# The router's early steps move ahead of the scores' minima in an attention and mixture-of-experts kernel

## The chip, the cores and the metric

One core of a Trainium2 chip runs the whole program. The metric is device microseconds of one execution, from start to end.

## What is computed

Attention over 8 batches and 8 heads with 576 positions of 64 numbers, a window of 128 positions and a bias that falls with the distance; its output, seen as 4608 tokens of 512 numbers, goes through a router that gives each token to one of 8 experts, and each expert is two matrix products with a ReLU between. The router sorts all (token, expert) logits downward and gives each token its expert while that has room:

```python
scores = np.where(mask, scale * np.matmul(q, k.transpose(0, 1, 3, 2)) + bias[None], -1000000000.0)
attn = np.exp(scores - np.max(scores, axis=-1, keepdims=True))
attn = attn / (np.sum(attn, axis=-1, keepdims=True) + 1e-09)
x = np.matmul(attn, v)          # as 4608 tokens x 512
...
logits = x @ w_gate             # 4608 x 8
for idx in np.argsort(-logits.flatten()):
    tok, e = (int(idx) // E, int(idx) % E)
    if assigned[tok] >= 0 or counts[e] >= cap:     # cap = 576
        continue
    assigned[tok] = e
    counts[e] += 1
...
h = np.maximum(x[mask] @ w1[e], 0.0)
out[mask] = h @ w2[e]
```

## The kernel before

`attention` runs over 32 pairs (a batch b and two heads), in a loop over n with four stages in each turn: the scores and minima of pair n, the turning of pair k = n - 2's weights, the product with `v` (`av`) of pair k - 1, and the last stage of pair k - 2. Nearly every instruction on TensorE (PE), VectorE and ScalarE is put in the order in which the code is written, so the order in the loop is the order in each engine's queue. One turn of the loop does, for the queues that matter here:

- VectorE: `least(n-1, 1)`, the minima of the second half of the scores (tile `u`, with the bias added); two copies `turned` of turned weights from PSUM into `PT`; `least(n, 0)`, the minima of the first half of the next scores; `divide(k-2)`, which makes `rs` (the reciprocals of the sums), `Lp` (parts of the logits) and `xb` (the output); and then, at the end, one early step of the router.
- PE: three turns into PSUM banks `pt`; `natural(k-2)`, which turns the product back and multiplies with the router's weights `wn`; the turns of tiles 0 and 4 into one more bank, for which PE waits until VectorE has copied the first `PT`; `scores(n, 0)`; `av(k-1)`; `scores(n, 1)`.
- ScalarE: the exponentials, one or two copies; GpSimd: sums `sd` of the denominators and, once per batch, the logits `L_sb` (lines L296 to L299).

The eight `pt`, `s` and `x` tiles fill PSUM: four banks `pt`, two `s`, two `x`.

The router needs all logits before it can choose, but parts of its work are done early. After batch b's logits, `early` puts generators on a list, and `early_step` takes one step of the first of them: `first_choice` in two halves (the best logit `b`, `ne` and `cand`; then its expert `am` and `OH`), and, once 27 of 36 token columns have their logits, `early_counts`: smallest and largest logit `ext`, their transpose on PE and `em`, `ed`; a matmul of `ed` that brings them to all partitions, and seven small instructions from `ev` to `hi`; the step width `w` and the places `kq`; then the indicator `ind` in three pieces and 13 matmuls that count. The steps fall in n = 8, 9, 12, 13, 16, 17, 20, 21, 24, 25, 28 and 29 (two halves for each of the six batches), n = 29 to 33 (`early_counts`); after n = 31 there are no more scores. In the profile all instructions of the steps have the line of the helper that records them, L446, and PE's matmuls L53.

Of the kernel before, what the change touches and what calls it, by code (L numbers as in the profile page):

```python
# [25 lines left out]
def attention(tc, pools, qk_in, v_in, rel_in, C, x_dram, L_sb, router):  # L26
# [25 lines left out]
    def mm(out, w, a, start=True, stop=True):  # L52
        put(nc.tensor.matmul(out, w, a, start=start, stop=stop, skip_group_check=True))  # L53

    def load(n):
        b, p = divmod(n, NP)
        t = sb.tile([128, QKW], F32, name="qk", bufs=3)
        nc.sync.dma_start(t, qk_in[b, p])
        state[n] = dict(q=t[:, 0:576], k=t[:, 576:1152])

    def load_v(n):
        b, p = divmod(n, NP)
        st = state[n]
        st["v"] = sb.tile([128, NB, 64], F32, name="v", bufs=4)
        nc.sync.dma_start(st["v"], v_in[b, p].rearrange("k (m c) -> k m c", c=64))

    def biases(p):

        bm[p] = pools["pp"].tile([128, BMW], F32, name=f"bm{p}")
        eng = nc.vector if p == 0 else nc.gpsimd  # L70
        for c0, c1 in ((0, 320), (320, 512)):
            for h in range(2):
                eng.tensor_scalar(bm[p][:, 512 * h + c0:512 * h + c1], rel[:, c0:c1], 2.0 ** -(2 * p + h + 1), 1.0, ALU.mult, ALU.mult)
            if c0 == 0:
                eng.tensor_scalar(bm[p][:, 1024:1216], rel[:, 0:192], rel[:, 512 + p:513 + p], 1.0, ALU.mult, ALU.mult)

    def unit(n, t):


        par = n // NP % 2  # L80
        m0, ms = 2 + par, 3 - 2 * par
        if t == 0:
            return m0, 0, 0, 320 if par else 192
        if t == 1:
            return 3, 64 * m0, 128 * m0, 0
        if t == 4:
            return ms, 64 * m0 + 192, 128 * m0 + 384, 1216 - 64 * ms
        return 3, 192 * (t - 2), 128 * m0 + 64 * ms + 384 * (t - 1), 0
# [9 lines left out]
    def keys(n, t, r):  # L98

        par = n // NP % 2  # L100
        qb = par + 2 * t + r if t < 4 else 8 - 8 * par
        if t == 0:
            return qb, 0, qb + 1
        return qb, max(0, qb - 2), min(3, qb + 1)

    def scores(n, half):
        st = state[n]
        q, k = st["q"], st["k"]
        if half == 0:
            st["u"] = sb.tile([128, 1600], F32, name="u", bufs=4)  # L110
            st["mn"] = sb.tile([128, 9], F32, name="mn", bufs=4)
            st["sm"] = sb.tile([128, 9], F32, name="sm", bufs=6)
        s = [bank() if half and n < 2 else ps_s.tile([128, 512], F32, name="s") for _ in range(2)]
        for t in UNITS[half]:
            m, c = unit(n, t)[0:2]
            w = 64 * m
            for h, r in HR if t < 4 else ((0, 0), (1, 1)):
                qb, kb, _ = keys(n, t, r)
                mm(s[h][hs[r], c:c + w], q[hs[h], 64 * qb:64 * qb + 64], k[hs[h], 64 * kb:64 * kb + w])
        st["s"] = s  # L120
# [41 lines left out]
    def turned(n, t, ps, copy):  # L162
        T = state[n][t] = sb.tile([128, 576], F32, name=f"PT{t}")
        w = 384 if t else place(n, 4, unit(n, 4)[0])
        put(copy(T[:, 0:w], ps[:, 0:w]))  # L165
# [43 lines left out]
    def copy_out(n):  # L209
        st = state[n]  # L210
        xT = st["xT"] = sb.tile([128, 640], F32, name="xT")
        for i, w in ((0, 320), (1, 256)):
            put(nc.scalar.copy(xT[:, 384 * i:384 * i + w], st["x"][i][:, 0:w]))

        nc.gpsimd.tensor_copy(xT[:, 320:384], xT[:, 256:320])

        st["sd"] = sb.tile([128, 10], F32, name="sd")
        add = nc.gpsimd.tensor_scalar
        add(st["sd"][:, 0:8], st["sm"][:, 0:8], 1e-9, 1.0, ALU.add, ALU.mult)
        for h in range(2):  # L220
            for r in range(2):
                add(st["sd"][hs[r], 8 + h:9 + h], st["sm"][hs[h], 8:9], 1e-9, 1.0, ALU.add, ALU.mult)
# [82 lines left out]
    NPAIRS = B * NP  # L305
# [7 lines left out]
    def bank():  # L313
        return ps_t.tile([128, 512], F32, name="pt")

    for n in range(NPAIRS + LAG + 2):
        if 0 < n < NPAIRS - 1:
            load(n + 1)
        if 0 < n <= NPAIRS:
            load_v(n - 1)  # L320
        if n == 2:
            nc.sync.dma_start(wn, C["wn_in"])
        if n == CONST_AT:
            load_consts(tc, pools["c"], C["cst_in"], C)
        if 0 < n < NP:
            biases(n)
        k = n - LAG
        turns, ends = 0 <= k < NPAIRS, 0 <= k - 2 < NPAIRS
        if ends:
            copy_out(k - 2)  # L330
        if 0 < n <= NPAIRS:
            least(n - 1, 1)
        if turns:
            ps = {}
            for t in (2, 1, 3):
                ps[t] = bank()
                turn(k, t, ps[t])
            turned(k, 2, ps[2], nc.scalar.copy)
        if 0 < n <= NPAIRS:
            exps(n - 1, 1)  # L340
        if turns:
            turned(k, 1, ps[1], nc.vector.tensor_copy)
            turned(k, 3, ps[3], nc.vector.tensor_copy)
            room = ps[3][:, 384:512]
        if k - 1 == NPAIRS - 1:
            av(k - 1)
        if ends:
            N = [bank(), bank()]
            natural(k - 2, N)
        if turns:  # L350
            ps = bank()
            turn(k, 0, ps)
            turn(k, 4, ps)
            turned(k, 0, ps, nc.scalar.copy)
        if n < NPAIRS:
            scores(n, 0)
            least(n, 0)
            exps(n, 0)
        if ends:
            divide(k - 2, N)  # L360
            if (k - 2) % NP == NP - 1 and k - 2 < NPAIRS - 1:
                logits((k - 2) // NP)
            if n < NPAIRS:
                router.early_step(room)
        if 0 <= k - 1 < NPAIRS - 1:
            av(k - 1)
        if n >= NPAIRS:
            for _ in range(1 if turns else 2):
                router.early_step(room if turns else None)
        if n < NPAIRS:  # L370
            scores(n, 1)

# [81 lines left out]
class Router:  # L454
# [24 lines left out]
    def bank(self):  # L479
        if self.room is not None:  # L480
            return self.room
        return self.p["ps_m"].tile([128, 512], F32, name="m")
# [116 lines left out]
    def early(self, c0, c1):  # L599

        choice = self.first_choice(self.L0, self.b0, self.am0, self.OH0, c0, c1)
        if c1 == NT:
            for steps in self.steps + [choice]:
                for _ in steps:
                    pass
            return
        self.steps += [iter([None]), choice]
        if c1 == FIRST:
            self.steps.append(self.early_counts())

# [11 lines left out]
    def early_counts(self):  # L622
        nc, rt, c1 = self.nc, self.p["rt"], FIRST - 1
        self.first = lo, w, rw = yield from self.ends(self.b0[:, 0:FIRST], True)
        self.clamp(self.c0, self.b0, lo, w, 0, c1)
        key = self.place(self.c0, lo, rw, 0, c1)
        ind = rt.tile([128, NT, J], BF, name="ind", bufs=1)
        yield
        for i in range(EARLY_CUTS):
            a, z = (c1 * j // EARLY_CUTS for j in (i, i + 1))  # L630
            self.indicate(ind, key, a, z)
        cnt = self.count(ind, self.OH0, 0, c1)
        t = self.small("pt", 8)
        nc.vector.tensor_copy(t[J:2 * J, :], cnt[0:J, 0:8])
        nc.vector.tensor_tensor(self.part[J:2 * J, :], cnt[J:2 * J, 8:16], t[J:2 * J, :], ALU.add)
# [328 lines left out]
def load_consts(tc, pool, cst, C):  # L964
    nc = tc.nc
    n = sum(w for _, w, _ in CONSTS)
    raw = pool.tile([128, n], F32, name="craw")
    nc.sync.dma_start(raw, cst)
    o = 0
    for k, w, dt in CONSTS:  # L970
        r = raw[:, o:o + w]
        if dt == F32:
            C[k] = r
        elif dt == BF:
            t = pool.tile([128, w], BF, name="c_" + k)
            nc.vector.tensor_copy(t, r)
            C[k] = t
        else:
            t = pool.tile([128, w, dt], BF, name="c_" + k)
            nc.vector.tensor_copy(t, bc(r.unsqueeze(2), [128, w, dt]))  # L980
            C[k] = t
        o += w
# [159 lines left out]
```

## Time and profile before

| | |
|---|---|
| Time, median of 3 runs | 717.23 us (717.13 to 718.87) |
| The profiled execution | 715.13 us, of which 713.4 us are the span from the first to the last instruction |
| Busy in the span: PE, VectorE, ScalarE, GpSimd | 679.1, 466.0, 331.1, 154.5 us |
| Attention | up to about 222 us |
| The router's first route, with PE mostly idle | from there to about 240 us |
| Experts | from there to the end |

The busy times are averages over parts with different limits. What a change in one part is worth is read in that part. PE's ends are modelled, so that PE's busy time is not PE at its peak.

### The profile page before, as it was taken

How to read it: one execution, taken by the hardware profiler on the slowest of the kernel's cores; microseconds unless marked ns; L12 is line 12 of the kernel's file. 1: busy time of each engine (PE TensorE's matmuls, PEld its weight loads, DVE VectorE, ACT ScalarE, POOL GpSimd, SP SyncE). 2: the span in 40 equal slices, each digit the busy share in tenths (PEclk: the TensorE clock that was granted, in tenths of full speed). 3: DMA queues.
4: the chain of work that ended last, by engine and by line, in shares of the span. 5: the costliest groups of instructions: out<-in, count | busy, mean ns of one | idle time of the engine just before them, and what ended most of it. 6: DMA issues, size and time to landing. Idle time of an engine off the chain costs nothing.

```text
span 713.4 us, 19210 instructions
## 1 busy us (share of the span) xinstructions
PE 679.1 (95%) x7447; PEld 596.6 (84%) x7447; DVE 466.0 (65%) x1855; ACT 331.1 (46%) x991; POOL 154.5 (22%) x337
## 2 busy tenths in 40 slices
PE   7999999999995699999999999999999999999996
PEld 4898888888874399789889889988988988988985
DVE  6778777877887789869578828846765724523210
ACT  6888888888873253324233223314324324322210
POOL 4121221221220301533042132132033023011011
PEclk9999999999997699999999999999999999999998
DMA  8465465465522352718135235135134334301001
GB/s 301 137 212 181 145 215 181 154 211 177 163 85 61 115 190 89 238 44 272 47 122 205 84 109 177 47 117 177 60 119 131 122 104 137 131 30 37 1 24 49
DMA packets 35140, 92.74 MB, mean 130 GB/s; under 512 B 3808, under 2 KB 13152, under 8 KB 35040
## 3 DMA queue, kind: packets, MB, share of 16 engines
q1 hardware_dynamic: 29152, 72.55, 31.0%
q0 software_dynamic: 5888, 18.88, 8.1%
q8 instruction: 61, 1.00, 0.6%
q14 instruction: 39, 0.32, 0.1%
HBM read 72.54 MB, written 18.87 MB: 128 GB/s over the span
## 4 chain that ended last, share of the span: by engine, by line
PE 76%; DVE 13%; DMA 4%; issue 4%; POOL 1%; SPq 1%; ACT 0%; POOLq 0%; DVEq 0%
PE ph L893 27%; PE po L922 10%; PE po L923 10%; PE po L925 8%; DVE u L133 6%; PE s L53 5%; PE pt L53 4%; PE pt L157 4%; PE x L53 3%; PE pg L870 2%; DVE xb L255 2%; PE m L579 1%; DMA craw<-in_cst_dram 1%; DVE PT L165 1%; DMA g<-x,idx 1%
## 5 line engine op out<-in xcount | busy, mean ns | idle before, releaser
L893 PE MATMUL ph<-xh,hl 128*128 128x288 f32 (+2 forms) x1024 | 192.0, 299 | 0.0
L893 PEld LDWEIGHTS ph<-xh,hl 128*128 128x128 f32 x1024 | 154.6, 189 | 1.0
L144 ACT ACTIVATE u<-u,mn 128x192 f32<-128x192 f32 (+2 forms) x288 | 123.8, 433 | 22.5 <-DVE mn L133 22.5
L922 PE MATMUL po<-hl,hh 128*128 128x512 f32 (+1 forms) x328 | 130.7, 399 | 0.0
L923 PE MATMUL po<-hl,hh 128*128 128x512 f32 (+1 forms) x328 | 126.4, 385 | 0.0
L893 PE MATMUL ph<-xl,hl 128*128 128x288 f32 (+2 forms) x512 | 115.9, 297 | 0.0
L899 ACT ACTIVATE hh<-ph 128x288 fp32r<-128x288 f32 (+2 forms) x128 | 46.6, 409 | 147.5 <-PE ph L893 141.4
L133 DVE CUSTOM_DVE_ANT_0 u<-s,bm 128x192 f32<-128x192 f32 x308 | 86.4, 333 | 39.5 <-PE s L53 39.0
L925 PE MATMUL po<-hl,hlo 128*128 128x512 f32 (+1 forms) x264 | 101.7, 385 | 0.0
L837 DVE TENSOR_TENSOR hl<-raw,hl 128x512 fp32r<-128x512 f32 x128 | 85.0, 683 | 14.4 <-ACT hl L835 13.9
L934 POOL DMA_INDIRECT out_dram<-o,idx x40 | 44.1, 1104 | 204.3 <-ACT o L929 120.9
L893 PEld LDWEIGHTS ph<-xl,hl 128*128 128x128 f32 x512 | 84.2, 189 | 0.1
L874 DVE TENSOR_TENSOR xl<-pg,xh 128x512 fp32r<-128x512 f32 (+1 forms) x37 | 23.7, 639 | 85.6 <-ACT xh L873 84.6
L904 DVE SCALAR_TENSOR_TENSOR hlo<-ph,hh 128x288 fp32r<-128x288 f32 (+2 forms) x128 | 49.5, 416 | 40.0 <-ACT hh L899 38.8
L835 ACT CAST hl<-raw 128x1024 fp32r<-128x1024 f32 x64 | 65.4, 1048 | 15.7 <-DMA raw<-in_w_dram 8.8
L53 PE MATMUL s<-qk 64*64 64x192 f32 (+1 forms) x1112 | 69.1, 319 | 2.0 <-DVE mn L133 1.7
L922 PEld LDWEIGHTS po<-hl,hh 128*128 128x128 f32 x328 | 61.7, 188 | 11.1
L923 PEld LDWEIGHTS po<-hl,hh 128*128 128x128 f32 x328 | 61.8, 188 | 10.7
L929 ACT COPY o<-po 128x512 f32<-128x512 f32 (+1 forms) x33 | 18.9, 574 | 96.1 <-PE po L925 62.1
L846 POOL DMA_INDIRECT g<-x,idx x40 | 45.1, 1126 | 81.9 <-PE pg L870 33.8
L157 PE MATMUL pt<-ident_sb,u 128*128 128x128 f32 x368 | 53.8, 281 | 7.3 <-DVE PT L165 6.0
L925 PEld LDWEIGHTS po<-hl,hlo 128*128 128x128 f32 x264 | 49.6, 188 | 10.3
(217 smaller groups left out, 931.9 us busy)
## 6 DMA issues: line engine op xcount, KB each, us to landing
raw<-in_w_dram SPq DMA_DIRECT2D x64, 512.0 KB, 4.3
qk<-in_qk_dram SPq DMA_DIRECT2D x32, 576.0 KB, 5.0
v<-in_v_dram SPq DMA_DIRECT2D x32, 288.0 KB, 3.8
x<-xb SPq DMA_DIRECT2D x14, 512.0 KB, 3.5
x<-xb SPq DMA_DIRECT2D x8, 128.0 KB, 2.6
x<-xb SPq DMA_DIRECT2D x4, 256.0 KB, 3.4
g<-x,idx POOLq DMA_INDIRECT x40
out_dram<-o,idx POOLq DMA_INDIRECT x40
```

The source lines that it names most:

```text
L53: put(nc.tensor.matmul(out, w, a, start=start, stop=stop, skip_group_check=True))
L133: put(nc.vector.tensor_tensor_reduce(out=u[rows], in0=x[rows, c:c + 64 * m].rearrange("q (j k) -> q j k", k=64), in1=bm[n % NP][rows, y:y ...
L144: put(nc.scalar.activation(u, u, AF.Exp, bias=st["mn"][:, i:i + 1], scale=-1.0, accum_out=st["sm"][:, i:i + 1]))
L157: put(nc.tensor.transpose(ps[:, c:c + 128], u[:, o + 128 * j:o + 128 * j + 128], ident))
L835: self.last = nc.scalar.copy(hl[:, 0, :], raw)
L837: nc.vector.tensor_tensor(hl[:, 1, c:c + 512], raw[:, c:c + 512], hl[:, 0, c:c + 512].bitcast(F32), ALU.subtract)
L893: nc.tensor.matmul(pp[t], w[:, a, j, fo:fo + 128], x[:, j, cut[t]:cut[t + 1]], start=(j == 0 and a == 0 and x is xh), stop=(j == 3 and a = ...
L899: nc.scalar.activation(o, pp[t], AF.Relu)
L904: nc.vector.scalar_tensor_tensor(d, pp[t][:, c0:c1], 0.0, o[:, c0:c1].bitcast(F32), ALU.max, ALU.subtract)
L922: nc.tensor.matmul(out, a, wh, start=(f == 0), stop=False)
L923: nc.tensor.matmul(out, a, wl, start=False, stop=(f == 7 and t == 4))
L925: nc.tensor.matmul(out, hl[:, f, 128 * t:128 * t + 128], wh, start=False, stop=(f == 7))
```

## The change

In iterations with scores the early step stands right behind VectorE's two copies, ahead of `scores(n, 0)` and `least(n, 0)`; before, it stood behind `divide`. `early_counts` yields once more, between the indicators and the count matmuls. The list of steps no longer gets an empty step ahead of each choice; the choice still begins in the iteration after its logits, as it was put on the list behind that iteration's step. In the last iterations, without turned weights, the steps get a free bank as their room.

```diff
@@ -353,6 +353,9 @@
             turn(k, 4, ps)
             turned(k, 0, ps, nc.scalar.copy)
         if n < NPAIRS:
+            if ends:
+
+                router.early_step(room)
             scores(n, 0)
             least(n, 0)
             exps(n, 0)
@@ -360,13 +363,11 @@
             divide(k - 2, N)
             if (k - 2) % NP == NP - 1 and k - 2 < NPAIRS - 1:
                 logits((k - 2) // NP)
-            if n < NPAIRS:
-                router.early_step(room)
         if 0 <= k - 1 < NPAIRS - 1:
             av(k - 1)
         if n >= NPAIRS:
             for _ in range(1 if turns else 2):
-                router.early_step(room if turns else None)
+                router.early_step(room if turns else bank()[:, 384:512])
         if n < NPAIRS:
             scores(n, 1)
 
@@ -604,7 +605,7 @@
                 for _ in steps:
                     pass
             return
-        self.steps += [iter([None]), choice]
+        self.steps += [choice]
         if c1 == FIRST:
             self.steps.append(self.early_counts())
 
@@ -629,6 +630,7 @@
         for i in range(EARLY_CUTS):
             a, z = (c1 * j // EARLY_CUTS for j in (i, i + 1))
             self.indicate(ind, key, a, z)
+        yield
         cnt = self.count(ind, self.OH0, 0, c1)
         t = self.small("pt", 8)
         nc.vector.tensor_copy(t[J:2 * J, :], cnt[0:J, 0:8])
```

On VectorE, the first half of a choice in one of the iterations where it stands (`PT` are the copies, L133 the minima, L248 and L255 the division; early steps have L446 before and L447 in the changed kernel, whose lines are moved by one):

```order
 L165 COPY PT_1015<-pt 128x384
 L165 COPY PT_1017<-pt 128x384
+L447 TENSOR_REDUCE b_73<-L_sb 128x4
+L447 TENSOR_TENSOR ne<-L_sb,b_73 128x8x4
+L447 SCALAR_TENSOR_TENSOR cand<-ne,c_eb 128x8x4
 L133 ISA u,mn<-s,bm_119 128x3x64
...
 L255 TENSOR_TENSOR xb<-pt,rs 128x2x128
-L446 TENSOR_REDUCE b_73<-L_sb 128x4
-L446 TENSOR_TENSOR ne<-L_sb,b_73 128x8x4
-L446 SCALAR_TENSOR_TENSOR cand<-ne,c_eb 128x8x4
 L133 ISA u,mn<-s,bm_119 128x2x64
```

The three instructions stand ahead of the first minima of the pair instead of behind its division.

On PE, the matmul of `ed` in n = 31 (behind the turns, `s<-qk` are the scores and `x<-PT,v` the product with `v`):

```order
 L157 MATMUL pt<-ident_sb,u 128x128 x3
 L53 MATMUL pt<-ident_sb,u 64x64 x2
+L447 MATMUL pt<-ed,craw 128x2
 L53 MATMUL s<-qk 64x192 x8
-L446 MATMUL pt<-ed,craw 128x2
 L53 MATMUL x<-PT_4075,v 64x128 x2
```

It stands ahead of the scores instead of behind them; the transpose of `ext`, in n = 30, is moved in the same way.

On VectorE, the end of attention before: the indicators of the early counts, the copy `pt` and sum `part` of the counts, the logits of pair 30 (`rs`, `Lp`) and the choice behind them.

```order
L446 TENSOR_TENSOR ind<-kq,c_i_425 128x512
L446 TENSOR_TENSOR ind<-kq,c_i_425 128x576 x2
L446 COPY pt<-pt 64x8
L446 TENSOR_TENSOR part<-pt 64x8
L240 RECIPROCAL rs<-sd 128x10
L248 TENSOR_TENSOR Lp<-pt,rs 128x3x2x8
L248 TENSOR_TENSOR Lp<-pt,rs 128x2x2x8
L446 TENSOR_REDUCE b_73<-L_sb 128x4
```

The same place in the changed kernel:

```order
L447 TENSOR_TENSOR ind<-kq,c_i_425 128x512
L447 TENSOR_TENSOR ind<-kq,c_i_425 128x576 x2
L240 RECIPROCAL rs<-sd 128x10
L248 TENSOR_TENSOR Lp<-pt,rs 128x3x2x8
L248 TENSOR_TENSOR Lp<-pt,rs 128x2x2x8
L447 COPY pt<-pt 64x8
L447 TENSOR_TENSOR part<-pt 64x8
L447 TENSOR_REDUCE b_73<-L_sb 128x4
```

The copy and the sum stand behind pair 30's `Lp`. On PE the 13 count matmuls stand between the two last `natural` instead of ahead of the last `av`.

## Rows read from the trace of the kernel before

**Rows 1.** Windows: us, busy (x) of PE, PEld, DVE, ACT, POOL; PEclk, DMA share, GB/s.

```profile
103.99:110.94 6.95, 6.44 (x133) 5.64 (x129) 5.57 (x30) 5.57 (x23) 1.19 (x6) 1.00 0.80 254
117.76:124.25 6.49, 6.49 (x140) 5.76 (x135) 5.06 (x27) 5.54 (x22) 1.19 (x6) 1.00 0.66 198
```

**Rows 2.** Waits, 0 to 224 us: us in total, times, longest.

```profile
DVE u L133 <- PE s L53: 39.0, 31, 1.5
PE pt L157 <- DVE PT L165: 6.0, 14, 0.7
```

**Rows 3.** Timeline of PE: turns that waited (start, us, work, idle before).

```profile
110.13 0.55 PE L157 MATMUL pt<-ident_sb,u 128*128 128x128 f32 x3 [0.51 <-DVE PT L165]
116.83 0.44 PE L157 MATMUL pt<-ident_sb,u 128*128 128x128 f32 x2 [0.27 <-DVE PT L165]
...
136.95 0.44 PE L157 MATMUL pt<-ident_sb,u 128*128 128x128 f32 x2 [0.52 <-DVE PT L165]
143.66 0.55 PE L157 MATMUL pt<-ident_sb,u 128*128 128x128 f32 x3 [0.26 <-DVE PT L165]
...
196.79 0.55 PE L157 MATMUL pt<-ident_sb,u 128*128 128x128 f32 x3 [0.43 <-DVE PT L165]
...
203.52 0.55 PE L157 MATMUL pt<-ident_sb,u 128*128 128x128 f32 x3 [0.40 <-DVE PT L165]
...
210.78 0.55 PE L157 MATMUL pt<-ident_sb,u 128*128 128x128 f32 x3 [0.73 <-DVE PT L165]
```

**Rows 4.** Timeline of VectorE: the free stretch, then a first half in its old place.

```profile
102.53 1.02 DVE L165 COPY PT<-pt 128x384 f32<-128x384 f32 x2
104.81 0.36 DVE L133 CUSTOM_DVE_ANT_0 u<-s,bm 128x192 f32<-128x192 f32 x1 [1.26 <-PE s L53]
...
107.19 0.20 DVE L446 TENSOR_REDUCE b<-L_sb 128x4 f32<-128x32 f32 x1
...
107.66 0.19 DVE L446 SCALAR_TENSOR_TENSOR cand<-ne,c_eb 128x32 bf16<-128x32 bf16 x1
107.77 0.28 DVE L133 CUSTOM_DVE_ANT_0 u<-s,bm 128x128 f32<-128x128 f32 x1
```

**Rows 5.** Timeline of GpSimd: the last sum of logits ahead of that step.

```profile
102.46 0.20 POOL L299 TENSOR_TENSOR L_sb<-by 64x8 f32<-64x8 f32 x1
```

**Rows 6.** Timeline of VectorE and PE: em and ed, ev to hi.

```profile
200.81 0.27 DVE L446 TENSOR_REDUCE em<-pt 2x1 f32<-2x128 f32 x1
201.30 0.34 DVE L133 CUSTOM_DVE_ANT_0 u<-s,bm 128x192 f32<-128x192 f32 x1
...
204.91 0.38 PE L446 MATMUL pt<-ed,craw 2*128 2x2 f32 x2
...
205.16 0.36 DVE L133 CUSTOM_DVE_ANT_0 u<-s,bm 128x192 f32<-128x192 f32 x1 [1.23 <-PE s L53]
...
207.53 0.15 DVE L446 COPY ev<-pt 128x2 f32<-128x2 f32 x1
...
208.56 0.35 DVE L133 CUSTOM_DVE_ANT_0 u<-s,bm 128x192 f32<-128x192 f32 x1
```

**Rows 7.** Timeline of PE and VectorE: the end of attention.

```profile
217.15 0.73 PE L446 MATMUL pt<-OH,ind 128*128 128x16 bf16 x13
...
217.92 0.16 DVE L446 COPY pt<-pt 64x8 f32<-64x8 f32 x1 [0.42 <-PE pt L446]
...
218.32 0.22 DVE L240 RECIPROCAL rs<-sd 128x10 f32<-128x10 f32 x1
...
220.95 0.20 DVE L446 TENSOR_REDUCE b<-L_sb 128x4 f32<-128x32 f32 x1
...
222.30 0.33 DVE L248 TENSOR_TENSOR Lp<-pt,rs 128x48 f32<-128x48 f32 x2
```

**Rows 8.** Two pieces of the chain that ended last (start, us, what).

```profile
204.33 0.74 PE s L53 x14
...
222.66 0.42 DVE L_sb L291
```

## The prediction, made before the change was run

> **What bounds the kernel now.** I read four things: the waits of the attention part, the granted clock and busy time by stretch, VectorE's rows around one early step, and the last microseconds of attention. The change touches only the first 223 us; the expert part behind them is one long chain that starts from what attention leaves, so I ask how much earlier that start comes.
>
> In attention TensorE (PE) is the limit. In the iteration from 117.76 to 124.25 us, which has no early step, PE is busy 6.49 us of 6.49; in the one from 103.99 to 110.94, which has one, it is busy 6.44 of 6.95, and the granted clock is full (2.4 GHz) in both [rows 1]. So PE stands still about half a microsecond there. The waits say for whom: over the whole of attention PE's turns of the weights waited for VectorE's copies `PT` 14 times, 6.0 us in total; VectorE in turn waited for PE's scores 31 times, 39.0 us in total [rows 2]. Both engines wait for each other in turn. Single waits of PE are 0.51 us behind the first half of a choice, 0.27 behind the second half, 0.40 behind `em`/`ed` and 0.73 behind `ev` to `hi` [rows 3]; the 14 are six pairs of halves (0.51 or 0.52, and 0.26 or 0.27, but 0.43 for the last second half, which also reduces `ext`) and the two singles.
>
> Why a step costs PE time is seen in VectorE's rows [rows 4]. The step's first instruction starts at 107.19 and the minima of the second half (`u`), which would stand in its place, at 107.77: 0.58 us later. VectorE's copies come right behind those minima, and PE waits for the copies. Ahead of the next scores' minima the same queue is empty: the copies that start at 102.53 last 1.02 us, and the minima behind them start at 104.81, after 1.26 us of waiting for PE.
>
> **The change part by part.** *Twelve halves of a choice (six batches).* Each goes from behind `divide` into the empty stretch ahead of the minima. It needs about 0.66 us there (from 107.19 to 107.85, the end of its last instruction), and 1.26 are free [rows 4], so the minima are not moved. VectorE gets back 0.58 us in the loop where PE stood still 0.51; a second half is two instructions, by the same spacing (0.47 us for the first two of three) some 0.35 us, against 0.27. The step is worth no more than PE's wait, since PE is full once that is gone. Sum of the twelve: 3 x 0.51 + 3 x 0.52 + 3 x 0.27 + 2 x 0.26 + 0.43 = 4.9 us, which is also 6.0 less the two singles (1.13).
>
> Does a half find its operands there? The first half reads the logits that GpSimd sums. In the new place it runs about 4 us sooner than in the old one. GpSimd's last sum starts at 102.46 and takes 0.20 us [rows 5]; VectorE is through with its copies at 103.55. That is 0.89 us to spare, so nothing is waited for.
>
> *`em` and `ed`.* Here the PE transpose of `ext` now stands ahead of the scores, and VectorE waits for it in front of the minima. The old cost on VectorE is 0.49 us (200.81 to 201.30) [rows 6], against a PE wait of 0.40. In the new place: transpose ends some 0.3 us after the turns, `em` and `ed` take 0.5, so they end at 0.8 to 0.9 us; the scores, behind a transpose of some 0.2 us (half of the 0.38 of two records [rows 6]), end at 0.74 [rows 8] + 0.2 = 0.94 us. The minima are then 0.2 us late, of which 0.09 is slack (0.49 less 0.40). Gain 0.3 us; bounds 0 (the round trip to PE and back is longer) and 0.4.
>
> *`ev` to `hi`, seven instructions.* Old cost 1.03 us (207.53 to 208.56) [rows 6], PE wait 0.73. In the new place `ev` can only start when the matmul of `ed` is done (two records, 0.38 us [rows 6]), some 0.5 us after the turns; the seven end at about 1.5 us, while before the minima started at 0.83 us (scores at 204.33 [rows 8], minima at 205.16 [rows 6]). So the minima are 0.7 us late; 0.30 is slack, 0.4 of PE's wait stays. Gain 0.3 us; bounds 0 and 0.73. Behind the waiting `ev` in VectorE's queue stand the four minima of that half; for them wait ScalarE's exponentials and the second scores on PE, which need the banks that the minima read. That VectorE takes them strictly in turn is shown at the end of attention, where the copy of the counts waited 0.42 us for PE and the reciprocal behind it started only afterwards [rows 7]. The Trainium skill, page "TensorE: Matmul & The Clock Gate", Part 1, says the same: ScalarE and VectorE are strict first-in-first-out queues, only PE pulls weight loads ahead. By that rule the sum keeps the 0.4 us loss; if the minima could pass the waiting `ev`, it would be 0.4 us better.
>
> *The step that yields once more (`early_counts`), and the removed empty step.* The empty step cost no instruction, and the first half of a choice stays in the iteration after its logits. The new yield puts the 13 count matmuls (0.73 us, from 217.15) behind the last but one `natural` instead of ahead of the last `av` [rows 7]. PE's work up to the last `natural` is the same, without a wait in it before or after: the last `av` starts 0.7 us sooner, the counts come some 3 us later. So PE ends at the same place. On VectorE the counts' copy and sum (217.92 to about 218.3) were done while it waited anyway; now they stand behind the `Lp` of pair 30 and ahead of the choice. That `Lp` used to end near 220.95 when the choice began; now it is earlier, but the counts end at about 220.7, so copy and sum run to some 221.15, the choice starts 0.2 us late, and so does the last `Lp`, at 222.30 before [rows 7]. Cost 0.2 us; bounds 0 and 0.7 (all of the counts' time shows). The chain that ended last passes through the row behind it, the last sum of logits at 222.66 [rows 8], so every gain or loss ahead of it reaches the end.
>
> *Banks.* The last steps now take two more `pt` banks per iteration; the second `natural` behind them waits for VectorE's counts copy, which ends while its first matmuls run. Nothing, bounded by the 0.4 us of copy and sum.
>
> **Sum.** 4.9 + 0.3 + 0.3 - 0.2 = 5.3 us. The profiled execution took 715.13 us (span 713.4 and 1.7 around it), 2.1 us under the median of the runs, 717.23; the three runs differ by 1.7 us among themselves. 715.13 - 5.3 is 709.8; off the median it is 717.23 - 5.3 = 711.9. Highest gain by the bounds: 6.0 us; lowest, with both singles at 0 and the tail at 0.7: 4.2 us.
>
> **The rivals.** *Half of it.* Where PE's wait goes, another wait that is now just behind shows: in a step iteration VectorE's slack after the change is only 0.07 us (0.58 less 0.51) for first halves and some 0.06 for second ones, and ScalarE is busy 5.54 of 6.49 us [rows 1]. If a step in the new place took some 1.5 us instead of 0.66, it would outlast the 1.26 us stretch and hold the minima for 0.2 us beyond the slack; fourteen times that is 2.8 us, and the gain falls to 2.5: 714.7. Against it: 0.6 us of the stretch stay free by the rows.
>
> *No change.* The time is given back behind attention, where the load of the first expert's weights or the gather sets a date of its own. Then 717. For it: DMA stands in the chain further on. Against: those loads are issued only when the route is known, so they move with it [rows 8]. Or PE's idle time is not there as its rows have it, since matmul ends are modelled; but the step iterations are longer by the same half microsecond [rows 1].
>
> *Slower.* The first halves now run some 4 us sooner, right behind GpSimd's sums. If these landed 3 us later than in the trace, VectorE would stand 3.0 - 0.89 = 2.1 us with the minima behind it, 0.6 of which the stretch still covers; six times 1.5 us is 9 us, less 5.3 is 3.7 slower: 721. It decides from sums that are 0.89 + 0.6 = 1.5 us late, and is a net loss from some 2.4 us. Nothing in the trace makes GpSimd late: its sums start from VectorE rows that the change leaves in place.
>
> **How the numbers follow.** Full gain 0.74 (its own range 710.4 to 713.8: the bounds 4.2 to 6.0 off 717.23, and 0.8 us either way, half the spread of the three runs), half 0.11, no change 0.11, slower 0.04. The time is that of the first, 711.9. For eight in ten the range takes the full gain and most of the half: 710.0 to 715.2. About 0.3% (2.1 us) is what a measurement of this kernel can tell from no change. Faster by more: 0.74 and nearly all of the half, 0.83; within: 0.13; slower by more: 0.04.
>
> **What would show it.** PE's waits for `PT` in attention fall from 14 and 6.0 us to one or two and under 0.7 us, the longest at the iteration with `ev`; VectorE's wait for scores shrinks by the steps' length in 12 iterations; step iterations last 6.4 to 6.5 us; the last sum of logits starts at about 217.4 in place of 222.66. Wrong would be: minima that start later behind a choice step, waits of VectorE for GpSimd at `b`, or an unchanged end with an earlier route.

## The result, and the profile after

The changed kernel takes 710.17 us (median of 4 runs, 708.85 to 713.08) against 718.05 us for the kernel before in the same comparison (717.13 to 718.87): a ratio of 0.991, 95% interval 0.9885 to 0.9936, or 4.6 to 8.3 us off 718.05. The forecast was 711.9 us; its range of 710.0 to 715.2 holds the time, by 0.2 us at its lower end. The gain of attention, 6.47 us in the stretch that the experiments below are read by, was larger than the 5.3 us of the sum and than the 6.0 that the forecast gave as its highest.

The windows of the same two iterations (n = 16, with a first half, and n = 18, with no step), in the columns of [rows 1]:

```profile
101.67:108.03 6.36, 6.36 (x132) 5.63 (x128) 5.63 (x31) 5.53 (x23) 1.19 (x6) 1.00 0.78 265
114.52:121.01 6.49, 6.49 (x140) 5.76 (x135) 5.06 (x27) 5.55 (x22) 1.19 (x6) 1.00 0.75 230
```

The iteration with a first half lasts 6.36 us instead of 6.95, and PE has no idle time in it. Its busy time fell too, from 6.44 to 6.36, which the prediction had not thought of.

The waits of the changed kernel, 0 to 220 us, that answer to [rows 2]:

```profile
DVE u L133 <- PE s L53: 29.8, 30, 1.4
DVE ev L447 <- PE pt L447: 0.7, 1, 0.7
```

There is no line left for PE's turns waiting for `PT`: the 14 waits and 6.0 us are gone, and PE's timeline from 50 to 190 us has no row with an idle time, where before it had those of [rows 3].

VectorE's timeline around a first half in its new place, as [rows 4], and then GpSimd's last sum ahead of it, as [rows 5]:

```profile
100.21 1.02 DVE L165 COPY PT<-pt 128x384 f32<-128x384 f32 x2
101.26 0.21 DVE L447 TENSOR_REDUCE b<-L_sb 128x4 f32<-128x32 f32 x1
101.50 0.19 DVE L447 TENSOR_TENSOR ne<-L_sb,b 128x32 bf16<-128x32 f32 x1
101.73 0.19 DVE L447 SCALAR_TENSOR_TENSOR cand<-ne,c_eb 128x32 bf16<-128x32 bf16 x1
102.49 0.36 DVE L133 CUSTOM_DVE_ANT_0 u<-s,bm 128x192 f32<-128x192 f32 x1 [0.57 <-PE s L53]
...
104.54 0.42 DVE L255 TENSOR_TENSOR xb<-pt,rs 128x256 f32<-128x256 f32 x1
104.87 0.28 DVE L133 CUSTOM_DVE_ANT_0 u<-s,bm 128x128 f32<-128x128 f32 x1
```

```profile
100.13 0.20 POOL L299 TENSOR_TENSOR L_sb<-by 64x8 f32<-64x8 f32 x1
```

The three instructions stand where VectorE waited for PE; of the 1.26 us of waiting 0.57 is left. Behind the division (L255) the second minima now follow at once. GpSimd's last sum ends at 100.33, 0.93 us ahead of `b`.

VectorE at `em`/`ed` and at `ev` to `hi`, as [rows 6]:

```profile
191.60 0.28 DVE L447 TENSOR_REDUCE em<-pt 2x1 f32<-2x128 f32 x1 [0.64 <-PE pt L447]
191.91 0.22 DVE L447 TENSOR_SCALAR ed<-ident_sb,em 2x2 f32<-2x2 f32 x1
192.53 0.36 DVE L133 CUSTOM_DVE_ANT_0 u<-s,bm 128x192 f32<-128x192 f32 x1 [0.40 <-PE s L53]
...
198.29 0.16 DVE L447 COPY ev<-pt 128x2 f32<-128x2 f32 x1 [0.74 <-PE pt L447]
...
199.24 0.16 DVE L447 TENSOR_TENSOR hi<-ev,sp 128x1 f32<-128x1 f32 x1
199.36 0.36 DVE L133 CUSTOM_DVE_ANT_0 u<-s,bm 128x192 f32<-128x192 f32 x1
```

`em` and `ed` delay nothing on VectorE: the minima behind them still wait 0.40 us for the scores. After `hi` they start with no wait.

The end of attention in the chain that ended last (start, us, what), as [rows 7, 8]:

```profile
198.25 0.81 PE s L53 x16
...
204.81 1.34 PE x L53 x54
...
213.20 0.40 PE pt L447 x13
...
213.62 0.17 DVE pt L447
...
213.82 0.17 DVE part L447
...
214.02 0.22 DVE b L447
...
215.74 0.42 DVE L_sb L291
```

The last sum of logits starts at 215.74 instead of 222.66, and the choice (`b`) now stands in the chain right behind the counts' copy and sum. The span fell from 713.4 to 708.7 us, 2.2 us less than the 6.92 by which the last sum came sooner; a second profile of the same kernel (below) shows what became of those.

### The profile page after: what moved, and what is told of

The parts are those of the page before. It is cut to its first block, busy times and chain, and to the rows that moved or that the text cites. A ratio compares the mean times of both kernels' runs of the same rounds, so it can differ in the third digit from the quotient of the medians.

```text
span 708.7 us, 19210 instructions
## 1 busy us (share of the span) xinstructions
PE 677.7 (96%) x7446; PEld 598.3 (84%) x7447; DVE 467.5 (66%) x1855; ACT 330.7 (47%) x991; POOL 154.1 (22%) x337
## 4 chain that ended last, share of the span: by engine, by line
PE 88%; DVE 5%; DMA 3%; issue 2%; POOL 1%; ACT 0%; SPq 0%; POOLq 0%; DVEq 0%
PE ph L895 28%; PE po L924 10%; PE po L925 10%; PE s L53 8%; PE po L927 8%; PE pt L53 7%; PE pt L157 6%; PE x L53 5%; PE pg L872 2%; DMA g<-x,idx 2%; PE m L580 1%; DVE u L133 1%; DMA raw<-in_w_dram 1%; DMA out_dram<-o,idx 1%; DMA rel_sb<-in_rel_dram 1%
## 5 line engine op out<-in xcount | busy, mean ns | idle before, releaser
L133 DVE CUSTOM_DVE_ANT_0 u<-s,bm 128x192 f32<-128x192 f32 x308 | 86.4, 333 | 30.2 <-PE s L53 29.8
L53 PEld LDWEIGHTS s<-qk 64*64 64x64 f32 x1112 | 48.2, 132 | 8.4 <-issue 3.7
```

The lines of the kernel that those rows point to most:

```text
L133: put(nc.vector.tensor_tensor_reduce(out=u[rows], in0=x[rows, c:c + 64 * m].rearrange("q (j k) -> q j k", k=64), in1=bm[n % NP][rows, y:y ...
```

## The experiments

All are read by one number, the *stretch*: from the start of the scores of n = 8, ahead of the first choice, to the start of the last sum of logits. It leaves out the start and the expert part, which differ between profiles by several microseconds for reasons of their own.

| kernel | scores n = 8 | last sum | stretch | last sum to end | median us (runs) | ratio to before, 95% |
|---|---|---|---|---|---|---|
| before | 51.01 | 222.66 | 171.65 | 490.7 | | |
| changed | 50.56 | 215.74 | 165.18 | 493.0 | 710.17 (4) | 0.991, 0.9885 to 0.9936 |
| e1 move only | 53.01 | 218.22 | 165.21 | 494.1 | 708.51 (6) | 0.9879, 0.9845 to 0.9913 |
| e2 yield only | 50.69 | 222.18 | 171.49 | 490.0 | 716.38 (12) | 0.9987, 0.9963 to 1.001 |
| e3 singles old | 54.43 | 220.32 | 165.89 | 491.0 | 710.56 (4) | 0.9901, 0.9863 to 0.9939 |
| e4 changed again | 50.56 | 215.73 | 165.17 | 490.6 | 708.66 (6) | 0.99, 0.9862 to 0.9938 |
| e5 double new | 50.65 | 216.00 | 165.35 | 489.7 | 709.22 (4) | 0.992, 0.9895 to 0.9945 |
| e6 double old | 50.73 | 228.95 | 178.22 | 489.3 | 720.54 (5) | 1.0076, 1.0048 to 1.0104 |
| e7 behind minima | 51.16 | 222.47 | 171.31 | 489.5 | 714.9 (10) | 1.0004, 0.9985 to 1.0023 |
| e8 choice ahead | 51.03 | 215.56 | 164.53 | 489.5 | 707.46 (4) | 0.9893, 0.9869 to 0.9917 |
| e9 triple new | 50.88 | 219.16 | 168.28 | 491.7 | 711.77 (10) | 0.9942, 0.9922 to 0.9962 |

(e1 to e4 and e5 to e8 each ran beside the kernel before on one chip: 716.22 and 714.79 us; e9 beside 715.6. The chain of e9 does not pass through its scores of n = 8; their start is put 0.31 us behind that of the timeline's row of them, as in before and changed.)

**Which of the two parts: e1 and e2.** e1 is the changed kernel without the new yield of `early_counts` (first diff, against changed); e2 (second diff, against before) is the kernel before with the yield alone, and the empty step kept except in the last batch, so that the choices stay where they were.

```diff
             self.indicate(ind, key, a, z)
-        yield
         cnt = self.count(ind, self.OH0, 0, c1)
```

> The steps are moved, but the early counts keep their place (no new yield). Measure: the stretch from the scores of n = 8 to the last sum of logits, 171.65 us before and 165.18 changed. Theory (VectorE's loop: a step costs what it takes on VectorE behind the division, and nothing in the stretch ahead of the minima): 171.65 - 6.3 = 165.3, about 6 us under the kernel before. Rival (the later counts are what gains): 171 or more, no change in time.

```diff
-                router.early_step(room if turns else None)
+                router.early_step(room if turns else bank()[:, 384:512])
...
-        self.steps += [iter([None]), choice]
+        self.steps += [choice] if c0 == FIRST else [iter([None]), choice]
...
             self.indicate(ind, key, a, z)
+        yield
```

> The early counts come later (new yield), the steps stay behind the division. Same stretch. Theory: only the end of attention moves, 0.1 to 0.2 us either way, 171.5; the time is that of the kernel before within 0.3%. Rival (the counts ahead of the last product held TensorE up): 3 us or more less, 168 or under.

Measured: 165.21 and 171.49 us. Without the yield the whole gain is there; the yield alone gives 0.16. The end of attention, from the last but one `av` to the last sum, takes 10.70 us in e1, 10.93 in changed, 11.07 before and 10.93 in e2. So the 0.14 by which changed is shorter there than before comes with the yield, wherever the steps stand, and e1's 0.37 with the removed empty step, which e1 has too: its choice comes one step sooner, so that the first half stands ahead of pair 30's `Lp`, in VectorE's wait for it:

```profile
214.23 0.21 DVE L447 TENSOR_REDUCE b<-L_sb 128x4 f32<-128x32 f32 x1
...
216.26 0.25 DVE L248 TENSOR_TENSOR Lp<-pt,rs 128x48 f32<-128x48 f32 x1 [1.24 <-PE pt L53]
```

In changed the new yield takes up that step, and the choice begins behind the counts and that `Lp`; this costs 0.23 us. In e1 the counts lie in the old place, and in the chain VectorE's choice no longer ends last:

```profile
213.15 0.65 PE pt L447 x13
213.79 1.50 PE s L53 x56
215.29 2.66 PE pt L53 x20
217.95 0.02 issue
217.98 0.23 DVE Lp L248
218.20 0.02 issue
218.22 0.42 DVE L_sb L291
```

That e1's stretch is not the shorter by these 0.23 us is a stall elsewhere: its PE stands 0.40 us up to 138.78, put down to "issue", in an iteration that lasts 6.56 us in place of 6.23. Less the end and this stall, the moved steps alone are worth some 6.3 to 6.4 us.

**What the two singles are worth: e3.** The changed kernel with the steps of n = 30 and 31 in the old place.

```diff
-            if ends:
+            if ends and n < 30:
                 router.early_step(room)
...
+            if 30 <= n < NPAIRS:
+                router.early_step(room)
```

> The changed kernel, but the steps of n = 30 and 31 (em and ed; ev to hi) stand behind the division as before. Same stretch. Theory: these two gave about 0.5 us, so 165.18 + 0.5 = 165.7. Rival (in the new place VectorE waits for TensorE with the minima behind it, and that costs what was gained): 165.2 or less.

Measured: 165.89 us, 0.71 more than changed, nearly all of it in n = 30 and 31 (14.15 us there against 13.45; 13.99 before). PE's two waits for `PT` are back:

```profile
PE pt L157 <- DVE PT L165: 1.3, 2, 0.9
```

So these steps pay in the new place too, although VectorE has to wait for PE in them.

**The microseconds lost behind attention: e4.** The changed kernel, unchanged, profiled a second time.

> The changed kernel once more. The stretch again 165.2. From the last sum of logits to the end of the span it was 490.7 us before and 493.0 changed. Theory (a chance stall of ScalarE and a lower clock behind it in the one profiled execution): 491 here, and a median about 6 us under the kernel before. Rival (the earlier start costs 2 us in the experts each time): 493 again, and a median 4 to 5 us under.

Measured: stretch 165.17, and 490.6 us from the last sum to the end in place of 493.0: the 2.3 us are not paid each time, as the theory had it. The waits of the expert part, first profile of changed, then the second:

```profile
PE pg L872 <- DMA g<-x,idx: 2.7, 2, 1.7
```

```profile
PE pg L872 <- DMA g<-x,idx: 0.9, 2, 0.6
```

In the first, PE waited 1.8 us longer for the gathers (before: 0.8 in all), and the granted clock of 365 to 400 us was 0.95 instead of 1.00. The gathers alone do not explain the loss: e7 waits 2.5 us for them and takes 489.5 us from the last sum to the end. The clock of 0.95 stands in changed and e1 alone, and these have the longest ends, 493.0 and 494.1 us; no row here shows the stall of ScalarE that the expectation names. In the four profiles with the halves behind the first minima (before, e2, e6, e7) the end takes 489.3 to 490.7 us, in the seven with them ahead 489.5 to 494.1. Whether the move makes the longer ones likelier is open. The span of the second is 706.3 us, 7.1 less than before's.

**Is the step free, and what is it worth: e5, e6 and e9.** The halves of the six early batches are computed two or three times, with the same result; e5 and e9 in the new place, e6 in the old.

```diff
-    def first_choice(self, L, b, am, OH, c0, c1):
+    def first_choice(self, L, b, am, OH, c0, c1, times=1):
...
+        for _ in range(times):
+            nc.vector.tensor_reduce(b, L.rearrange("p e c -> p c e"), AX.X, ALU.max)
+            nc.vector.tensor_tensor(ne[:, :, 0:n], L, bc(b.unsqueeze(1), [128, 8, n]), ALU.is_lt)
+            nc.vector.scalar_tensor_tensor(cand[:, :, 0:n], ne[:, :, 0:n], -16.0, eb, ALU.mult, ALU.add)
...
+        for _ in range(times):
+            nc.vector.tensor_reduce(am, cand[:, :, 0:n].rearrange("p e c -> p c e"), AX.X, ALU.max)
+            nc.vector.tensor_tensor(OH, eb, bc(am.unsqueeze(1), [128, 8, n]), ALU.is_equal)
...
-        choice = self.first_choice(self.L0, self.b0, self.am0, self.OH0, c0, c1)
+        choice = self.first_choice(self.L0, self.b0, self.am0, self.OH0, c0, c1, 2 if c0 < FIRST else 1)
```

(3 in place of 2 in e9.)

> The changed kernel with the five instructions of a choice done twice, for the six batches in the loop (same results). Measure: from the scores of n = 8 to the last sum of logits, 165.18 us changed. Theory (the stretch ahead of the minima has 0.7 us left): 0.70 and 0.47 us more fit or nearly fit, 165.2 to 165.6. Rival (the stretch is not free, VectorE's work counts wherever it stands): 6 x (0.70 + 0.47) = 7.0 more, 172.

> The kernel before with the same doubling, the steps behind the division. Same stretch, 171.65 us before. Theory (there every microsecond of VectorE counts): 171.65 + 7.0 = 178.7. Rival (a step's cost there is a fixed one, a wait or a hand-over, not its work): 171.7 to 173.

> The halves of the choices of the six early batches are done three times (same result), in the new place. What the stretch from the scores of n = 8 to the last sum of logits shows: 165.2 us in the changed kernel, 165.35 with the halves done twice, where no wait of VectorE is left ahead of the minima behind a doubled first half (0.57 us were left with a single one) and 0.26 us behind a doubled second half. Theory (the halves are free only as long as they fit into VectorE's wait for the scores; past that each microsecond of VectorE costs one of TensorE): a third first half, 0.57 us, is paid in full six times, a third second half, 0.49 us, less 0.26 six times, so 165.35 + 3.4 + 1.4 = 170.2 us, and TensorE waits for PT again about 0.5 and 0.2 us, twelve times. Rival (the minima have slack of their own behind that wait, since nothing waits for their first result at once): under 167.5 us. For comparison: three times in the old place, by 0.57 and 0.49 us for each further one, would be 178.2 + 6.4 = 184.6 us.

Measured: doubling costs 0.17 us in the new place and 6.57 in the old one. The 0.17 are about what e5 loses in n = 11, an iteration without a step (6.84 us against 6.66). PE's waits in e6, and one of them in its timeline:

```profile
PE pt L157 <- DVE PT L165: 12.6, 14, 1.1
```

```profile
112.71 0.55 PE L157 MATMUL pt<-ident_sb,u 128*128 128x128 f32 x3 [1.09 <-DVE PT L165]
```

A second copy of the first half adds 0.57 us to the iteration (7.52 from 106.00 to 113.52, against 6.95) and 0.58 to the wait (1.09 against 0.51, [rows 3]), all that VectorE spends on it; so there was no slack between the two. In e5 the same copy stands in what was left of VectorE's wait and uses it up; behind the second half 0.26 is left:

```profile
102.56 0.19 DVE L447 SCALAR_TENSOR_TENSOR cand<-ne,c_eb 128x32 bf16<-128x32 bf16 x1
102.74 0.36 DVE L133 CUSTOM_DVE_ANT_0 u<-s,bm 128x192 f32<-128x192 f32 x1
...
109.11 0.36 DVE L133 CUSTOM_DVE_ANT_0 u<-s,bm 128x192 f32<-128x192 f32 x1 [0.26 <-PE s L53]
```

The third copy of e9 is past the end of that room, and is paid: 2.93 us more than e5, between the 4.8 of the theory and what the rival allowed. In n = 8 the iteration with the first half is 0.52 us longer (6.89 against 6.37), close to the 0.57 expected, and so in two more of the six; in the other three it is 0.37 or 0.38. The one behind it, with the second half, is only 0.04 longer (6.53 against 6.49), where 0.23 was expected. PE's timeline shows another wait than expected, from n = 8 on in the six iterations with a first half and in no other; two of the six:

```profile
105.35 1.37 PE L53 MATMUL s<-qk 64*64 64x128 f32 x20 [0.43 <-DVE mn L133]
131.85 1.27 PE L53 MATMUL s<-qk 64*64 64x192 f32 x20 [0.26 <-DVE mn L133]
```

It is the second scores that wait for the minima, not the turns for `PT`: the bank that the prediction named behind `ev` becomes the limit when minima start late. A lateness of some 0.2 us is nearly swallowed there; one of 0.57 costs 0.37 to 0.52. So for the first halves the theory holds in the main, though not by the wait that it named, and for the second halves the rival does.

**Where in the queue: e7.** The kernel before with the steps a little further forward, behind the first minima and ahead of the division, with the rest of the change.

```diff
             least(n, 0)
             exps(n, 0)
+            if ends:
+                router.early_step(room)
...
-            if n < NPAIRS:
-                router.early_step(room)
```

> The changed kernel with the step between the first minima and the division: earlier than before, but not in the stretch in which VectorE waits for the scores. Same stretch, 171.65 before and 165.18 changed. Theory (only that stretch is free): no gain, 171.5 with the later counts. Rival (what helps is that the step no longer stands behind the division): 165.2 to 167.

Measured: 171.31 us, 0.34 under before, ratio 1.0004. Being earlier, or on the other side of the division, is worth little; ahead of those four minima is worth all. PE waits as in before, by 0.51 and 0.26 behind the halves (14 waits, 5.6 us).

**The choice out of the chain's end: e8.** The changed kernel with the last but one batch's choice taken ahead of pair 30's division.

```diff
+            if n == NPAIRS + 1:
+                for _ in router.last_choice:
+                    pass
             divide(k - 2, N)
...
-        self.steps += [choice]
+        if c0 == FIRST:
+            self.last_choice = choice
+        else:
+            self.steps += [choice]
```

> The changed kernel with the last batch but one's choice (five instructions, 1.1 us) ahead of pair 30's division, in the 1.9 us in which VectorE waits for it. Same stretch. Theory: the chain at the end of attention loses the choice and is then bound by TensorE: 165.18 - 0.3 = 164.9. Rival (the copy of the counts and its sum hold the last logits up just as well): 165.2.

Measured: 164.53 us, 0.65 under changed, twice the 0.3 of the theory. The tail from `av` to the last sum takes 10.37 us; PE ends the chain there, as in e1, and the five instructions of the choice stand where VectorE would wait for `natural`:

```profile
213.58 0.38 PE pt L450 x13
213.97 1.32 PE pt L53 x10
215.29 0.02 issue
215.31 0.23 DVE Lp L248
215.54 0.02 issue
215.56 0.42 DVE L_sb L291
```

Its median, 707.46 us, is 1.07% under before, the shortest of all kernels measured here. Against changed (0.991 and 0.99) the intervals overlap: that it is the faster rests on the stretch, not on the times.

## Why the prediction was right, and where it was off

*The mechanism held.* Steps behind the division cost PE time because VectorE's copies come later; ahead of the next minima they lie in VectorE's wait. e1 and e2 put all but the end's 0.14 us on the move, e5 and e6 show the two places' prices for the same instructions (0.17 and 6.57 us), e7 that the place alone decides. The rival of *half* the gain needed steps that outlast the wait: e9 shows that this rival's mechanism exists, from about 1.25 us a half on, and that the steps of the change, at 0.66, are half as long.

*The twelve halves: 5.8 us, not 4.9.* From the scores of n = 8 to the turns' end of n = 30 the changed kernel takes 140.80 us (191.36 less 50.56), before 146.59 (197.60 less 51.01). The step that failed is "The step is worth no more than PE's wait, since PE is full once that is gone." The first four halves' iterations shrank by 0.57, 0.33, 0.62 and 0.34 us, close to the 0.58 and 0.35 that the prediction itself gave as VectorE's cost, while PE's rows showed 0.51, 0.27, 0.52 and 0.26 idle. The 0.07 between them is in the first window above: PE's busy time fell from 6.44 to 6.36 for the same work. PE "full" at 6.44 was not its floor. That the rows count some waiting as busy because the ends of matmuls are modelled fits this, but no run here separates it.

*`em`/`ed` and `ev` to `hi`: 0.54 us together, against 0.6.* n = 30 shrank by 0.15 (6.73 to 6.58), n = 31 by 0.39 (7.26 to 6.87). The way of reckoning held, but both sizes were off, in opposite directions, so that the sum comes so close is in part luck. Counted from the end of the turns, the minima started at 0.83 us before; now they start at 1.17 behind `ed` (192.53 less 191.36) and at 1.42 behind `hi` (199.36 less 197.94). They are 0.34 and 0.59 us late, where 0.2 and 0.7 were forecast. Less the slack of 0.09 and 0.30 that the prediction gave, 0.25 and 0.29 us of the gain are lost by that; 0.15 of the 0.40 and 0.44 of the 0.73 remain, near what was measured. The round trip of `em` is hidden; what makes these minima late is that PE's transpose stands ahead of the scores.

What the forecast had wrong is where the rest shows. No row has the 0.4 us of wait that were to stay: PE's idle time is gone but for 0.03 us, and its busy time rose instead. n = 30 and 31 before, and then changed, in the columns of [rows 1]:

```profile
197.60:204.33 6.73, 6.33 (x138) 5.48 (x133) 5.39 (x29) 5.54 (x22) 1.19 (x6) 1.00 0.14 46
204.33:211.59 7.26, 6.53 (x138) 5.64 (x134) 6.08 (x36) 5.64 (x22) 2.47 (x11) 1.00 0.27 93
```

```profile
191.36:197.94 6.58, 6.58 (x133) 5.86 (x132) 5.43 (x29) 5.54 (x23) 1.19 (x6) 1.00 0.24 74
197.94:204.81 6.87, 6.84 (x139) 6.19 (x142) 6.17 (x36) 5.58 (x23) 2.47 (x11) 1.00 0.28 98
```

The rise is about that of the second scores, 20 matmuls, which take 0.98 and 0.93 us with these steps behind the division (in before, and again in e3) and 1.27 and 1.26 in the new place; why is not shown. VectorE did keep the order: the scores were done at 199.06, and the minima stood behind the waiting `ev` and `hi` until 199.36, as the rule cited from the Trainium skill's page "TensorE: Matmul & The Clock Gate", Part 1, says.

*The tail: 0.14 us gained, against 0.2 lost.* The order came out as described: counts, copy and sum, choice, last `Lp`. But the 13 count matmuls hold PE for 0.40 us in the new place and not 0.73 [rows 7] (0.67 in the chain of before), so the choice starts 9.21 us behind `av` (214.02 less 204.81) instead of the 9.56 forecast (9.36 before and 0.2). The moved steps have no part in this: e2, with the steps in the old place, has the same end of 10.93 us. The prediction took the removed empty step as free of cost and gain; by e1 it would be worth 0.37 us here, of which the yield takes back 0.23.

*All of it reaches the end.* The last sum was forecast for 217.4 and starts at 215.74: 1.2 us from the terms above (5.8, 0.54 and 0.14, together 6.47, against 5.3), and 0.45 because attention itself started earlier in that profile. e4 shows that it goes through to the end, so the rival of *no change* behind attention falls. The rival of *slower* needed late sums of GpSimd; they had 0.93 us to spare, against 0.89 forecast.

*The time.* The forecast took 717.23 as the time before; in the comparison it was 718.05, and 714.79 to 716.22 in the later ones. By the ratio the gain is 4.6 to 8.3 us; 5.3 and the stretch's 6.47 both lie in it, so it is the stretch, not the times, that shows the sum to be short.

## What to carry to other kernels

In an in-order queue the place of a short step matters more than its length: look for the wait that the engine has anyway, measure it, and put the step ahead of the instruction that waits, not behind work that the other engine needs next. When two engines wait for each other in turn, price a step at what it takes on the engine that runs it (0.58 here), not at the idle time seen on the other (0.51): in this kernel PE's busy time changed with the waits, down in one iteration (6.44 to 6.36) and up in others (6.33 to 6.58). Doubling the disputed instructions in both places is a cheap test of whether they are hidden; tripling them shows where the cover ends, and which resource is next.

## What was not expected of the hardware

The start of attention differs by up to 3.9 us between these profiles (scores of n = 8 at 50.56 to 54.43), and the granted clock goes with it. Windows of e3 (6 to 20 us), in the columns of [rows 1]:

```profile
6.00:12.00 6.00, 4.96 (x79) 3.56 (x78) 5.94 (x39) 4.54 (x21) 5.33 (x14) 1.00 0.99 359
12.00:20.00 8.00, 6.22 (x58) 4.59 (x59) 4.18 (x25) 5.94 (x27) 2.29 (x12) 0.57 0.63 237
```

From 12 to 20 us e3 was granted 0.57 of full speed and e1 0.59, a mean near the lower of the two levels (1.2 GHz); the other nine kept 1.00. PE had been busy 4.96 and 5.12 us of the 6 ahead of it in these two, 3.77 and 4.72 in changed and before, but 5.36 in e7, so this does not tell them apart. e3 and e1 start 3.9 and 2.4 us later than changed. What decides it was not tested.

The 13 count matmuls take 0.40 us behind `natural`'s long matmuls and 0.65 to 0.67 behind `av`'s short ones (e8 and e2: 0.38 and 0.40; e1 and before: 0.65 and 0.67). But e6 has them behind `av` too, and there they take 0.49, so the place alone does not decide. Whether the weight loads or the indicators make the difference was not tried.
